# Second weights of two experts loaded by column halves, output stored by halves and in larger pieces

## The chip, the cores and the metric

The kernel runs on one core of one Trainium2 chip. A core has five engines with their own instruction streams: TensorE (PE; its weight loads are listed as PEld), VectorE (DVE), ScalarE (ACT), GpSimd (POOL) and SyncE (SP). Transfers between the chip's memory (HBM) and the core's SBUF are run by 16 DMA engines; POOL issues this kernel's loads (queue q0 in the profile), SP its stores (queue q1). TensorE writes to PSUM, which has eight banks of 128 partitions x 2 KB.

The metric is the device time of one execution in microseconds. "Before" is a median of three runs.

## The reference

Two stages, on float32 inputs.

```python
# attention: q, k, v are (8, 8, 576, 64)
scores = scale * q @ k.T                  # per batch and head
scores = where(masks[head], scores, -1e9) # heads 0-3: last 32 positions
attn = softmax(scores)                    # heads 4-7: every 4th of the last 128
x = (attn @ v).transpose(0, 2, 1, 3).reshape(4608, 512)

# soft mixture of experts: phi (512, 32), w1 (8, 512, 1024), w2 (8, 1024, 512)
logits = x @ phi                          # 32 slots, 4 for each of 8 experts
slot_input = softmax(logits, axis=0).T @ x
for e in range(8):
    h = np.maximum(slot_input[e] @ w1[e], 0.0)
    slot_out[e] = h @ w2[e]               # (4, 512)
out = softmax(logits, axis=1) @ slot_out  # (4608, 512) float32
```

Every slot's input is a sum over all 4608 tokens, and every output row needs all 32 rows of `slot_out`. So the last stage, `out`, can begin only when attention is done for all tokens and the last expert's `w2` has been used. Columns of `out` depend on the same columns of `w2` alone.

## The kernel before

The kernel doesn't write its instructions in their final order. It describes operations (`op`), each with its engine, what it reads and writes, an estimated cost and a key, and a planner (`Prog.schedule`, L149) places them: on PE, ACT and DVE by the earliest possible start in its own model of time and, among starts within 0.12 us of each other, by key; on POOL and SP in the order in which they were described. Each engine then works through its list in order and waits on semaphores. The planner's model has one line for all transfers, in which each takes its bytes over 424 GB/s after those placed before. In the modelled stretch `FILL` it fills PE's gaps with matmuls of no use (L1022).

Attention runs in eight units, each two batches by four heads; its code is not touched. During it POOL loads q, k and v, and, as their buffers come free, the weights: `w1` of experts 0 to 6 into `WD`, then `w17`, `w20` to `w24` into the three staging buffers `stg`, then `w25`, `w26` and `w27` into `TT` (`wload`, L428; L766 to L768). A weight is 2 MB of float32 and is written as 1 MB of bf16: 128 partitions with 8 KB each, for `w2` eight chunks of 512 columns. A load may be split into parts by chunks, each with a semaphore of its own: `w27` is split at chunks 4, 6 and 7. After the weights come fifteen transfers of a few bytes (`mk`, L773).

After attention: `fo` and `siT` (the slot inputs, L785), the first layer into `h_sb` (L805 to L815), its transpose `hT` (L823), the row sums of the tokens' weights and their reciprocals `rtok` (L842, L847). `expT` holds the 4608 tokens' exponentials, token by column, with the 32 slots in 4 groups of 8 rows at partitions 0, 32, 64 and 96.

The second layer, `ffn2` (L880), adds into the PSUM pair `sp_`, one bank for each half of 256 columns: experts 0 to 3, 4 to 6, chunks 0 to 3 and 4 to 5 of expert 7, each for half 0 and then half 1. The sum so far, without chunks 6 and 7 of expert 7, is scaled into `so_sb` by DVE (L906) and ACT (L910). For the first 512 tokens the output starts from this incomplete sum (L941), and the missing chunks are added by matmuls with `G` (L943), which holds those tokens' weights times the hidden values of chunks 6 and 7, computed beforehand (L859 to L873). Meanwhile `ffn2` adds chunks 6 and 7 for all others; the complete slot output is `so_all`: POOL copies rows 0 to 95 from `so_sb` (L913), DVE and ACT scale rows 96 to 127 (L962, L966).

The output goes by groups of 256 tokens, partition p taking tokens 2p and 2p + 1 of the group: two matmuls of 512 columns into a PSUM pair (L990), one evacuation with scaling by `rtok` on ACT (L1002) and one on DVE (L1001), into buffers of weights no longer needed, and one store of 512 KB by SP (L977). The first group is evacuated and stored as two stores of 256 KB. In memory a partition's share of a store is one run of 4 KB (2 KB in the first group).

Of the kernel before, what the change touches and what calls it, by code (L numbers as in the profile page):

```python
# [65 lines left out]
class Pool:  # L66
# [38 lines left out]
    def use(self, tile, op):  # L105
        for i in tile.phys:
            self.last[i].append(op)
# [194 lines left out]
def bass_dilated_sliding_attn__then__soft_moe_slots_kernel(  # L302
# [45 lines left out]
    so_sb = sb("so_sb", [128, DM])  # L348
    m7 = sb("m7", [128, 1], F32)
# [6 lines left out]
    psum = Pool(8, {1: [[6]] + one[:6], 2: [[0, 1], [2, 3], [4, 5], [6, 7]]})  # L356
# [40 lines left out]
    b_m7, b_soa = Buf(), [Buf(), Buf(), Buf()]  # L397
# [24 lines left out]
    def home(ap, al, name):  # L422
        b = Buf()
        b.al = al
        HOME[name] = (ap, b)
        b_home.append((ap, b))

    def wload(name, parts=((0, 8),)):  # L428
        ap, b = HOME[name]
        e = int(name[2:])  # L430
        src = (moe_w1 if name[:2] == "w1" else moe_w2)[e]
        c = 4 if name[:2] == "w1" else 8
        v_ = src.rearrange("(p c) f -> p c f", c=c)
        d_ = ap.rearrange("p (c f) -> p c f", c=c)
        b.parts = []
        for i, (lo, hi) in enumerate(parts):
            lo_, hi_ = lo * c // 8, hi * c // 8
            sem = DmaSem(nc, f"s_{name}_{i}")
            pb = Buf()
            for al in b.al:  # L440
                pb.prev = pb.prev + al.ready + al.reads
            o = op("pool", lambda g, lo_=lo_, hi_=hi_: [g.dma_start(d_[:, lo_:hi_], v_[:, lo_:hi_])],  # L442
                   after=pb.prev, a=[pb], cost=0.6, sem=sem, nbytes=2097152 * (hi - lo) // 8)
            b.parts.append((lo, hi, pb))
            b.ready.append(o)
# [321 lines left out]
    wload("w26")  # L767
    wload("w27", ((0, 4), (4, 6), (6, 7), (7, 8)))  # L768
# [66 lines left out]
    NOG = N_TOK // 256  # L835
    tok = [expT[:, 256 * o:256 * o + 256].rearrange("p (t j) -> p j t", j=2) for o in range(NOG)]
    rs = tile(psum, 1)

    def rsum(t):
        for o in range(NOG):  # L840
            for j in range(2):
                i_ = t.matmul(bank(rs)[:, 2 * o + j:2 * o + j + 1], tok[o][:, j], rowm[:],  # L842
                              start=True, stop=True)
        return i_
    op("pe", rsum, r=b_expT + [b_rowm], w=[rs], alloc=[rs], cost=1.0, key=K1 + 1,
       after=[ffn1])
    op("dve", lambda vv: vv.reciprocal(rtok[:], bank(rs)[:, 0:2 * NOG]), r=[rs], w=[b_rtok],  # L847
# [6 lines left out]
    h7, t_soa = tile(pPT), tile(pPT)  # L854
    G = [tile(pPT), tile(pPT)]

    def so_all(p0=0, p1=128, sl=slice(0, 512)):
        return sbt(t_soa)[p0:p1, sl]
# [16 lines left out]
    sp_ = tile(psum, 2)  # L875
    b_sp = [Buf(), Buf()]

    chain = []

    def ffn2(es_, lo, hi_, h_, key):  # L880
        pbs = [pb for e in es_ for l2, h2, pb in HOME[f"w2{e}"][1].parts
               if l2 < hi_ and h2 > lo]

        def pe(t):
            for cc in range(lo, hi_):
                for e in es_:
                    j, hi = e % 4, e // 4
                    i_ = t.matmul(pair(sp_)[32 * j:32 * j + 32, h_, 0:256],
                                  hT[:, hi, cc, j, :],
                                  w2v[e][:, cc, 256 * h_:256 * h_ + 256],  # L890
# [3 lines left out]
        o = op("pe", pe, r=[b_hT[0], b_hT[1]] + pbs, alloc=[] if chain else [sp_],  # L894
               a=[sp_, b_sp[h_]], cost=0.12 * (hi_ - lo), mode="c", key=key, after=chain[-1:])
# [4 lines left out]
    for es_, lo, hi_ in (((0, 1, 2, 3), 0, 8), ((4, 5, 6), 0, 8), ((7,), 0, 4), ((7,), 4, 6)):  # L900
        for h_ in range(2):
            ffn2(es_, lo, hi_, h_, K1 + 2 + es_[0] + 0.1 * lo + 0.02 * h_)
    for h_ in range(2):
        sl = slice(256 * h_, 256 * h_ + 256)
        if h_ == 0:
            op("dve", lambda vv, sl=sl: vv.tensor_scalar(so_sb[:, sl], pair(sp_)[:, 0, 0:256],  # L906
                                                         rcs[:, 0:1], None, op0=AluOp.mult),
               r=[b_sp[0], b_rcs, sp_], w=[b_so[0]], cost=0.35, key=K1 + 20)
        else:
            op("act", lambda ac, sl=sl: ac.activation(so_sb[:, sl], pair(sp_)[:, 1, 0:256],  # L910
                                                      ACTF.Copy, scale=rcs[:, 0:1]),
               r=[b_sp[1], b_rcs, sp_], w=[b_so[1]], cost=0.4, key=K1 + 20)
    op("pool", lambda g: g.tensor_copy(so_all(0, 96), so_sb[0:96, :]), r=b_so, w=[b_soa[0], t_soa],  # L913
       alloc=[t_soa], cost=1.0, key=K1 + 21)

    osts = []
    for ap, b in b_home[:9]:
        t32 = ap.bitcast(F32).rearrange("p (n j f) -> p n j f", n=2, j=2)
        for n_ in range(2):
            osts.append((t32[:, n_], b))  # L920

    PO = []
    NGT = NG // 256

    def Gt(o, c):
        return sbt(G[c])[:, 256 * o:256 * o + 256].rearrange("p (t j) -> p j t", j=2)
    pb7 = {l2: pb for l2, h2, pb in HOME["w27"][1].parts}
    PO = [[tile(psum, 2), tile(psum, 2)], tile(psum, 2)]
    head = {}

    def first(c, key):
        for o in range(2):
            for j in range(2):
                po = PO[0][j] if o == 0 else PO[1]

                def pe(t, o=o, j=j, po=po):
# [138 lines left out]
```

## Time and profile before

| What | Value |
|---|---|
| median of three runs (lowest, highest) | 182.53 us (182.01, 182.73) |
| span of the profiled execution | 180.5 us |
| busy: PE, DVE, ACT, POOL | 133.5, 114.9, 93.7, 44.9 us |
| read from HBM, written to HBM | 61.94 MB, 9.44 MB |
| loads, 100 to 136 us: written to SBUF | 216 GB/s |
| stores, 158 to 178 us | 405 GB/s |
| granted TensorE clock, mean | 0.956 |

The span is from the first to the last instruction of one profiled execution. The runs are timed around the whole launch, so they are longer by what lies before the first and after the last instruction; the profiled execution has no such time of its own, and its span is what stands beside the runs. The load rate counts the bf16 bytes that are written; the float32 bytes read are twice as many. These rows are from the costliest groups of instructions (line, engine, operation, out<-in, shape, count | busy us, mean ns | idle before) between 150 and 181 us:

```profile
L1001 DVE TENSOR_SCALAR WD<-ps,rtok 128x512 f32<-128x512 f32 x13 | 8.7, 740 | 0.8 <-PE ps L943 0.8
```

```profile
L1002 ACT ACTIVATE WD<-ps,rtok 128x512 f32<-128x512 f32 x13 | 7.6, 725 | 0.8 <-PE ps L943 0.8
L1002 ACT ACTIVATE stg<-ps,rtok 128x512 f32<-128x512 f32 x4 | 2.6, 728 | 0.0
```

### The profile page before, as it was taken

To read this page: it belongs to the slowest core of one execution; us is meant where nothing else is said; L and a number is where in the kernel's file an instruction comes from. 1 tells how busy PE (TensorE), PEld (TensorE's weight loads), DVE (VectorE), ACT (ScalarE), POOL (GpSimd) and SP (SyncE) were. 2 spreads that over 40 slices of the span, in tenths; PEclk is the share of its full clock that TensorE was granted. 3 is DMA by queue.
4 is the path that set the end of the run, shared out by engine and by line. 5 is a ranking of instruction groups with operands and counts; after the bars stand their busy time and mean duration, and the time that the engine had idled before them with its cause. 6 is when DMAs were issued, how large, how long until landed. Compare 5 with 4: busy or idle time off the path is not lost.

```text
span 180.5 us, 5811 instructions
## 1 busy us (share of the span) xinstructions
PE 133.5 (74%) x2597; PEld 99.2 (55%) x2597; DVE 114.9 (64%) x263; ACT 93.7 (52%) x138; POOL 44.9 (25%) x90
## 2 busy tenths in 40 slices
PE   0019769967988989888986898798999966995000
PEld 0019659656768767568865677775646654411000
DVE  6840495894797798688699179789840501799000
ACT  2004867945767975675975374874410301797000
POOL 7990702501600701700200200016970001000000
PEclk9999999999999999999999699999999999999655
DMA  5999999999999999999999999999999993499998
GB/s 72 196 219 206 220 210 212 218 212 216 214 214 219 211 216 214 214 216 212 216 213 212 218 214 218 216 216 214 212 221 212 216 188 53 155 404 406 403 406 318
DMA packets 8808, 40.81 MB, mean 226 GB/s; under 512 B 2384, under 2 KB 2640, under 8 KB 5328
## 3 DMA queue, kind: packets, MB, share of 16 engines
q0 software_dynamic: 5520, 30.94, 83.5%
q1 hardware_dynamic: 3264, 9.50, 13.5%
q8 instruction: 20, 0.33, 0.7%
q14 instruction: 4, 0.03, 0.0%
HBM read 61.94 MB, written 9.44 MB: 395 GB/s over the span
## 4 chain that ended last, share of the span: by engine, by line
PE 31%; DVE 26%; DMA 19%; ACT 9%; issue 4%; POOL 2%; DVEq 0%; POOLq 0%
DMA TT<-in_moe_w_dram 14%; DVE XB L644 7%; DVE PT L594 7%; PE ps L542 6%; DMA stg<-in_v_dram 5%; DVE WD L1001 5%; PE ps L537 5%; PE ps L688 4%; ACT TT L561 4%; ACT PT L586 4%; DVE VN L609 4%; PE ps L604 4%; PE ps L661 3%; PE ps L579 3%; PE ps L633 3%
## 5 line engine op out<-in xcount | busy, mean ns | idle before, releaser
L561 ACT ACTIVATE TT<-ps 128x864 f32<-128x864 f32 x32 | 28.6, 895 | 32.0 <-PE ps L542 23.1
L586 ACT ACTIVATE PT<-ps 128x768 bf16<-128x768 f32 x48 | 36.6, 815 | 6.3 <-PE ps L579 5.9
L644 DVE TENSOR_TENSOR XB<-ps,RV 96x768 bf16<-96x768 f32 x32 | 30.3, 947 | 0.7
L542 PE MATMUL ps<-ident,stg 96*64 96x96 bf16 x576 | 17.9, 225 | 17.1 <-DMA stg<-in_v_dram 13.0
L542 PEld LDWEIGHTS ps<-ident,stg 96*64 96x64 bf16 x576 | 15.8, 124 | 18.6 <-DMA stg<-in_v_dram 13.0
L609 DVE COPY VN<-ps 128x768 bf16<-128x768 bf16 x32 | 17.5, 547 | 10.5 <-PE ps L604 10.5
L413 POOL DMA_DIRECT2D stg<-in_q_dram x16 | 8.5, 536 | 44.5 <-PE ps L542 23.8
L633 PE MATMUL ps<-VN,PT 128*128 128x65 bf16 x384 | 17.7, 194 | 2.0 <-DVE PT L594 0.9
L673 DVE COPY XT<-ps 128x576 bf16<-128x576 bf16 x17 | 10.1, 597 | 12.2 <-PE ps L661 12.2
L604 PE MATMUL ps<-ident,TT 128*128 128x128 bf16 x192 | 16.5, 221 | 1.9 <-issue 1.1
L633 PEld LDWEIGHTS ps<-VN,PT 128*128 128x128 bf16 x384 | 14.5, 98 | 4.4 <-DVE PT L594 1.7
L579 PE MATMUL ps<-TT 64*128 64x96 bf16 x384 | 15.2, 204 | 1.9 <-ACT TT L561 1.0
L661 PE MATMUL ps<-ident,XB 96*128 96x96 bf16 x192 | 12.9, 208 | 3.2 <-DVE XB L644 3.0
L537 PE MATMUL ps<-ident,stg 96*128 96x96 bf16 x288 | 14.9, 206 | 0.1
L604 PEld LDWEIGHTS ps<-ident,TT 128*128 128x128 bf16 x192 | 11.0, 98 | 5.9 <-issue 2.6
L594 DVE TENSOR_TENSOR PT<-PT,mask_d 128x768 bf16<-128x768 bf16 x24 | 13.0, 544 | 0.9 <-ACT PT L586 0.4
L537 PEld LDWEIGHTS ps<-ident,stg 96*128 96x128 bf16 x288 | 13.0, 98 | 0.3 <-ACT PT L586 0.3
L661 PEld LDWEIGHTS ps<-ident,XB 96*128 96x128 bf16 x192 | 9.8, 99 | 6.0 <-DVE XB L644 4.9
L442 POOL DMA_DIRECT2D stg<-in_moe_w_dram x6 | 3.2, 534 | 39.4 <-PE ps L537 26.4
L579 PEld LDWEIGHTS ps<-TT 64*128 64x128 bf16 x384 | 9.6, 94 | 5.9 <-ACT TT L561 1.1
L594 DVE TENSOR_TENSOR PT<-PT,mask_p 128x768 bf16<-128x768 bf16 x24 | 12.6, 538 | 0.0
L674 ACT ACTIVATE XT<-ps 128x576 bf16<-128x576 bf16 x15 | 9.7, 649 | 3.7 <-PE ps L661 3.5
(92 smaller groups left out, 193.5 us busy)
## 6 DMA issues: line engine op xcount, KB each, us to landing
WD<-in_moe_w_dram POOLq DMA_DIRECT2D x7, 1024.0 KB, 28.0
out_dram<-WD SPq DMA_DIRECT2D x13, 512.0 KB, 5.0
stg<-in_moe_w_dram POOLq DMA_DIRECT2D x6, 1024.0 KB, 23.1
stg<-in_q_dram POOLq DMA_DIRECT2D x16, 288.0 KB, 17.9
stg<-in_k_dram POOLq DMA_DIRECT2D x16, 288.0 KB, 19.7
stg<-in_v_dram POOLq DMA_DIRECT2D x16, 288.0 KB, 21.6
TT<-in_moe_w_dram POOLq DMA_DIRECT2D x2, 1024.0 KB, 20.8
out_dram<-stg SPq DMA_DIRECT2D x4, 512.0 KB, 5.1
```

The costliest lines, as they stand in the source:

```text
L537: i_ = t.transpose(bankb2(pt, a)[:, 96 * kk:96 * kk + 96], two[:, j // 2, c, :], ident[0:96, 0:96])
L542: i_ = t.transpose(bankb2(pt, a)[64 * hx:64 * hx + 64, 96 * kk:96 * kk + 96], src[:, hx, c, :], ident[0:96, 0:96])
L561: return ac.activation(d, sv, ACTF.Copy)
L579: i_ = t.matmul(pair(sc)[:, hx, QB * x:QB * x + QB], win(u, 1, h01, blk_, bpar)[64 * hx:64 * hx + 64], win(u, 0, h01, blk_, bpar)[64 * hx: ...
L586: op("act", lambda ac: ac.activation(sbt(pt)[:, 0:768].rearrange("p (x n) -> p x n", x=2), pair(sc)[:, :, 0:384], ACTF.Exp, scale=SCALE), ...
L594: return dv.tensor_tensor(p_, p_, m.unsqueeze(1).to_broadcast([128, 2, 384]), AluOp.mult)
L604: i_ = t.transpose(bankb(pv)[:, 128 * m:128 * m + 128], win(u, 2, h01, m, bpar), ident[:, :])
L609: op("dve", lambda dv: dv.tensor_copy(sbt(vn)[:, :, :, 0:64], bankb(pv)[:, 0:768].rearrange("p (m x d) -> p m x d", m=6, x=2)), r=[pv], w= ...
L633: i_ = t.matmul(pair(po)[:, bk, 65 * po_:65 * po_ + 65], sbt(pts[i])[:, o_:o_ + 128], sbt(vn)[:, m, half, 0:65], start=True, stop=True)
L644: op("dve", lambda dv: dv.tensor_tensor(sbt(xb)[:].rearrange("p m (x h d) -> p h x m d", x=2, h=2)[:, h01], pv()[:, :, :, 0:64], sbt(rv)[: ...
L661: i_ = t.transpose(bankb(px)[:, QB * m:QB * m + QB], sbt(xb)[:, m, 128 * x:128 * x + 128], ident[0:QB, 0:QB])
L673: return en.tensor_copy(d, s_)
```

## The change

`w26` and `w27` are loaded by column halves: first columns 0 to 255 of `w26`, then of `w27` (chunks 0 to 5, then 6 to 7), then the same for columns 256 to 511. A part now names chunks and columns, and `ffn2` waits for the parts that meet its own.

The order of the second layer is experts 0 to 3 and 4 to 5 for both halves, then expert 6 and chunks 0 to 5 of expert 7 for half 0, then `half(0, ...)`, then the same for half 1. `half` scales the sum so far into `so_sb`, makes the output of the first 512 tokens as before (incomplete sum, then `G`), adds chunks 6 and 7, completes `so_all` for its columns, and evacuates and stores its 256 columns of the first six groups of 256 tokens (`NAB = 6`). The remaining 3072 tokens go at full width in groups of 512, 512, 1024 and 1024, one store each; a partition then takes 4 or 8 tokens in a row.

In the half stores a partition's share is two runs of 1 KB; in the others it is one run of 8 or 16 KB. In the loads by halves a chunk is a run of 1 KB that is read and 512 B that are written. `so_all` lies in the bytes of `psA_sb` in place of a tile of the `PT` ring, and bank 7 of PSUM joins the single banks. Stores of the first part are issued by SP in the order half 0, groups 0 to 5, half 1, groups 0 to 5.

```diff
-    wload("w26")
-    wload("w27", ((0, 4), (4, 6), (6, 7), (7, 8)))
+    for h_ in range(2):
+        sl = (256 * h_, 256 * h_ + 256)
+        wload("w26", ((0, 8) + sl,))
+        wload("w27", ((0, 6) + sl, (6, 8) + sl))
...
+    NAB = 6
+    GRP = [2] * NAB + [4, 4, 8, 8]
...
-    for es_, lo, hi_ in (((0, 1, 2, 3), 0, 8), ((4, 5, 6), 0, 8), ((7,), 0, 4), ((7,), 4, 6)):
...
+    def half(h_, key):
+        sl = CH[h_]
+        eA, eB = (("dve", "act"), ("act", "dve"))[h_]
+        xe = op(eA, lambda en: scaled(en, so_sb[:, sl], bank(sp_[h_])[:, 0:256], rcs[:, 0:1]),
+           r=[b_sp[h_], b_rcs, sp_[h_]], w=[b_so[h_]], cost=0.45, key=key)
+        op("pool", lambda g: g.tensor_copy(so_all(0, 96, sl), so_sb[0:96, sl]), r=[b_so[h_]],
+           w=[b_soah[h_][0]], after=b_psA.ready + b_psA.reads, cost=0.6, key=key + 0.1)
+        po = [tile(psum, 1) for _ in range(3)]
...
+        for c in (None, 0, 1):
+            for o in range(2):
+                for j in range(2):
...
+                        if c is None:
+                            return t.matmul(d_, row(d0, 2)[j], so_sb[:, sl],
...
+                        return t.matmul(d_, sbt(G[c])[:, d0 + j:d0 + 256:2], w2v[7][:, 6 + c, sl],
+                                        start=False, stop=c == 1, skip_group_check=True)
...
+        ffn2((7,), 6, 8, h_, key + 3.5, after=[xe])
...
+        for j in range(2):
+            op(("act", "dve")[j], lambda en, j=j: scaled(
+                en, AB[0][1][:, j, sl], bank(po[j])[:, 0:256], rtok[:, j:j + 1]),
+               r=[po[j], b_rtok], a=[ob], after=prev, cost=0.4, key=key + 4)
+        store(d0, 2, ap, ob, key + 4, h_)
+        op(eB, lambda en: scaled(en, so_all(96, 128, sl), bank(sp_[h_])[96:128, 0:256],
+                                 rcs[96:128, 0:1]),
...
+        for o in range(1, NAB):
...
+                    for j in range(2):
+                        i_ = t.matmul(bank(p2)[:, CH[j]], row(d0, 2)[j], so_all(0, 128, sl),
+                                      start=j == 0, stop=True, skip_group_check=True)
...
+            kr = rtok[:, 2 * o:2 * o + 2].unsqueeze(2).to_broadcast([128, 2, 256])
...
+                return dv.tensor_tensor(ap[:, :, sl], bank(p2).rearrange("p (j f) -> p j f", j=2),
+                                        kr, AluOp.mult)
+            if o % 2 == 0 or o == 1:
+                op("dve", evd, r=[p2, b_rtok], a=[ob], after=prev, cost=0.65, key=key + 4 + o)
+            else:
+                for j in range(2):
+                    op("act", lambda en, ap=ap, p2=p2, j=j, o=o: scaled(
+                        en, ap[:, j, sl], bank(p2)[:, CH[j]], rtok[:, 2 * o + j:2 * o + j + 1]),
+                       r=[p2, b_rtok], a=[ob], after=prev, cost=0.4, key=key + 4 + o)
+            store(d0, 2, ap, ob, key + 4 + o, h_)
+
+    for es_ in ((0, 1, 2, 3), (4, 5)):
+        for h_ in range(2):
+            ffn2(es_, 0, 8, h_, K1 + 2 + es_[0] + 0.02 * h_)
+    ffn2((6,), 0, 8, 0, K1 + 10)
+    ffn2((7,), 0, 6, 0, K1 + 11)
+    half(0, K1 + 20)
+    ffn2((6,), 0, 8, 1, K1 + 30)
+    ffn2((7,), 0, 6, 1, K1 + 31)
+    half(1, K1 + 40)
+
+    for i, (n, hs) in enumerate(((4, (3,)), (4, (4,)), (8, (5, 6)), (8, (7, 8)))):
...
+        for j0 in range(0, n, 2):
+            po = tile(psum, 2)
...
+                for j in range(2):
+                    i_ = t.matmul(pair(po)[:, j, :], row(d0, n)[j0 + j], so_all(), start=True, stop=True)
...
+            for j in range(2):
+                op(("act", "dve")[j], lambda en, ap=ap, po=po, j=j, j0=j0, n0=n0: scaled(
+                    en, ap[:, j0 + j, :], pair(po)[:, j, :], rtok[:, n0 + j0 + j:n0 + j0 + j + 1]),
+                   r=[po, b_rtok], a=[ob], after=prev, cost=0.6, key=key)
+        store(d0, n, ap, ob, K1 + 70 + 10 * i)
```

## The prediction

> **What bounds the kernel now.** I read the page's 40 slices first, because two rows there answer the question by themselves.
>
> ```profile
> DMA  5999999999999999999999999999999993499998
> GB/s 72 196 219 206 220 210 212 218 212 216 214 214 219 211 216 214 214 216 212 216 213 212 218 214 218 216 216 214 212 221 212 216 188 53 155 404 406 403 406 318
> ```
>
> The DMA row is full from slice 1 to 32 (loads; GB/s counts the bf16 bytes that are written, half of the f32 bytes read) and again from slice 35 on (stores, 404 GB/s). Between them is one hole. The kernel is a stream of transfers, so a change is worth what it does to that hole and to the work in the stream. A table of 1 us stretches shows the hole's size (columns: PE, PEld, DVE, ACT, POOL busy, clock, DMA share, GB/s):
>
> ```profile
> 148.00:149.00 1.00, 1.00 (x36) 0.95 (x30) 0.00 (x0) 0.00 (x0) 0.00 (x0) 1.00 0.96 144
> 149.00:150.00 1.00, 0.47 (x14) 0.18 (x6) 0.00 (x0) 0.00 (x0) 0.00 (x0) 1.00 0.59 99
> 150.00:151.00 1.00, 0.91 (x8) 0.57 (x6) 0.00 (x0) 0.00 (x0) 0.00 (x0) 1.00 0.72 103
> 151.00:152.00 1.00, 0.61 (x4) 0.30 (x4) 0.20 (x1) 0.20 (x1) 0.00 (x0) 1.00 0.20 20
> ...
> 154.00:155.00 1.00, 1.00 (x7) 0.45 (x6) 0.97 (x3) 0.97 (x3) 0.00 (x0) 1.00 0.00 0
> 155.00:156.00 1.00, 1.00 (x6) 0.49 (x5) 0.24 (x2) 0.17 (x2) 0.00 (x0) 1.00 0.86 324
> 156.00:157.00 1.00, 1.00 (x7) 0.42 (x5) 1.00 (x2) 1.00 (x2) 0.00 (x0) 1.00 0.53 201
> 157.00:158.00 1.00, 1.00 (x5) 0.24 (x4) 1.00 (x3) 1.00 (x3) 0.00 (x0) 1.00 0.47 193
> 158.00:159.00 1.00, 0.94 (x4) 0.23 (x4) 1.00 (x2) 1.00 (x3) 0.00 (x0) 1.00 1.04 418
> ```
>
> Missing share, from 148 to 158: 0.04 + 0.41 + 0.28 + 0.80 + 0.98 + 1.00 + 1.00 + 0.14 + 0.47 + 0.53 = 5.7 us. That is the most that filling it could give. What makes it is the chain of work between the last weights and the first store, in order of time:
>
> ```profile
> 151.15 0.61 PE L888 MATMUL ps<-TT,hT 128*32 128x256 bf16 x4 [0.24 <-DMA TT<-in_moe_w_dram]
> ...
> 151.80 0.48 DVE L906 TENSOR_SCALAR so_sb<-ps,rcs 128x256 bf16<-128x256 f32 x1 [7.40 <-PE ps L888]
> ...
> 152.43 0.60 PE L941 MATMUL ps<-so_sb,expT 128*128 128x256 bf16 x4 [0.67 <-DVE so_sb L906]
> ...
> 152.86 1.04 PE L943 MATMUL ps<-TT,PT 128*128 128x256 bf16 x8
> ...
> 153.72 0.88 DVE L1001 TENSOR_SCALAR WD<-ps,rtok 128x256 f32<-128x256 f32 x2 [1.44 <-PE ps L943]
> ...
> 154.29 16.68 SPq L977 DMA_DIRECT2D out_dram<-WD  x15
> ```
>
> From the landing at 151.10 (PE goes at 151.15) to the first store's issue at 154.29 is 3.2 us; its first packet follows at 155.14 (+0.85), its landing at 156.35.
>
> **The slow engine's ledger.** The landing records hold 16 increments for each transfer, one for each DMA engine. In the loads the engines have drifted apart: w25 is complete on the first at 138.57 and on the last at 141.73, the last part of w27 on 148.47 and 152.38. A consumer waits for the last, so I keep the books of the slowest engine: w25 done 141.73, loads done 152.38, the fifteen tiny mk transfers (0.17 us apart) until 154.93, stores from 155.14. For it most of the 5.7 us is not idle: a gap of at most 2.8 us (152.38 to 155.14) and about 0.9 us around 157, 3.7 us in all. Its end closes: the third store's first packet at 157.53 + 17 stores x 1.287 us + 0.6 us from last packet to landing = 180.0; measured 180.04, and the span ends 0.46 us later.
>
> **Part 1: column halves of the weights.** Removed: 8 packets of 8192 B on each engine for w26, and 8 of 4096, 8 of 2048, 16 of 1024 for w27 (sizes as written). Added: 256 packets of 512 B (2 MB / 512 / 16 engines), in six transfers for five. No packet of 512 B stands in the trace. On the first engine the spacing of landings is 4.88, 2.44, 1.25 and 0.66 us for 8 packets of 8192, 4096, 2048 and 1024 B: 610, 305, 156, 82 ns a packet, a line of 0.072 ns/B and 8 ns. At 512 B the line gives 45 ns, and 42 without the completion write (a 4-byte record of 22 ns for each group of 8, rare among 64); I take 43. Bounds: 38 ns (the 8192 B rate, no cost), and 60 ns from the packets' recorded durations (98, 173, 324, 625 ns, which overlap their neighbours by 15 ns; the line goes to 60). Loads: 256 x 43 = 11.0 us for 9.9 (4.88 + 2.44 + 1.25 + 2 x 0.66), +1.1; bounds -0.1 to +5.5. The Trainium skill ("Advanced Engine Details and Errata", Clock Domains) has 42 to 43 ns for a descriptor of 1 KiB, which is what each of these reads; by that the sum is 10.9 us, and no run here shows it yet. POOL issues 22 transfers instead of 21, at the 0.5 us of its rows; it is idle from 134 to 152 and the data are 14 us behind the issues, which hides slower issuing too. If it did not, each us late would delay the loads by one.
>
> **Part 2: stores by halves, and larger ones.** Twelve stores of 256 KB in 1 KB pieces: 192 packets an engine. Stores of 2048 and 4096 B record 86 and 164 ns (0.038 ns/B and 9 ns): 47 ns at 1 KB, 9.0 us. Bounds: 41 ns (rate of 4096 B), 7.9 us, and 86 ns (a piece of 1 KB as dear as one of 2 KB), 16.5 us; I take the line, since 128 B packets of phi record 13 ns, near it. The rest, 3072 tokens, has pieces of 8 and 16 KB: 8 x (2 x 315 + 2 x 620) ns = 15.0 us for 12 x 1.287 = 15.4; bounds 14.9 and 15.4. Before, all stores took 2 x 0.69 + 17 x 1.287 = 23.3 us; after, 24.0. The Trainium skill ("Trace Analysis", DMA Optimizations) speaks against this part: transfers under 2 KB carry a significant overhead and should be batched. In "DMA: Bandwidth & Descriptors" (Anatomy of one DMA) it is priced as 2.0 us + bytes / 436 GB/s for each, 2.6 us for one of these and 31 us for twelve in a row. The trace's own pair of 256 KB stores landed at 156.35 and 157.00, 0.65 us apart, so the 2 us overlap here and the row decides.
>
> **Part 3: compute that moves.** The first half's chain now starts when w27's chunks 0 to 6 of columns 0 to 256 have landed. It is the old chain: two more L888 matmuls (0.2 us), the 0.48 us scaling, 4 + 8 matmuls, one 0.48 us evacuation: 3.4 us. The six groups' evacuations are, on DVE, one 128x256 (0.48) and three 128x512 by tensor_tensor (not in the trace on this shape; between the 740 ns of L1001 and the 947 ns of L644's 96x768), on ACT 128x256 pieces at 0.47: about 3 us a half, against 4.5 us of transfer: hidden. If it were not, each us would be a us of empty queue, once a half. The GpSimd copy (0.61 us for 512 columns) is done twice, beside the evacuations. From then on a pair of tiles costs 0.74 us against 1.25 us of transfer, hidden.
>
> **The sum, slow engine.** Half 0 of the loads: 141.73 + 5.5 + 0.4 (half of the 0.75 us by which the last engine's loads exceeded the first's) = 147.6, chunks 0 to 6 at 146.9. First store issued 150.3, first packet 151.15. Of half 1's 5.9 us, 2.35 are then left, 1.6 of chunks 0 to 6. How an engine shares itself between the load queue and the store queue no row shows: bounds are that the loads lose nothing, and that they wait for all of the half-0 stores (4.5 us); I take turns about, packets being of like cost. Then chunks 0 to 6 land at 151.15 + 2 x 1.6 = 154.35, all at 155.85, and of the 4.5 us of half-0 stores 2.15 are left, until 158.0. The second chain ends in a first packet at 154.35 + 3.4 + 0.85 = 158.6: a hole of 0.6 us remains where 3.7 were. Then 4.5 + 15.0 = 19.5 us: 178.1, + 0.6 landing + 0.4 = **span 179.1**, 1.4 below 180.5. The median of the runs, 182.53, is 2.0 above the profiled span; I keep that difference: **181.1 us**. Check as a difference: holes -3.1, loads +1.1, stores +0.7 = -1.3. With the loads losing nothing the hole closes and the time is 180.5; with loads waiting for all stores, chunks 0 to 6 land at 157.25, first packet 161.5, span 182.0, time 184.0.
>
> **Rivals.** *Nothing measurable.* PE takes its work in the planner's order. Where that puts the half-1 matmuls of experts 6 and 7 ahead of groups 2 to 5 of half 0, those four wait for the half-1 landing; PE already waits so at 147.41 and 149.86 before L888. Then only two stores run beside the loads, which land (chunks 0 to 6) near 154.1; the four come 1 us of matmuls and evacuation later, first packet 156.2 (+0.85), run until 159.2, then 19.5 + 1.0: span 179.7, time 181.7. For it: the planner's transfers never share an engine, so it expects half 1 early. Against: it also counts each group as ready about when the weights are.
>
> *Slower: the 512 B packet.* Place: half 1 of the loads. If a packet costs the recorded 60 ns, half 0 takes 7.7 + 0.4 us, chunks 0 to 6 land at 148.8, the first store packet at 153.05; 3.9 us of half-1 chunks 0 to 6 remain and by turns land at 160.85; by then the half-0 stores are almost used up, the queue is empty from 162 to 165.1, and 165.1 + 19.5 + 1.0 = span 185.6, time 187.6. Between 43 and 60 ns the end moves 0.38 us a ns, so the sign turns near 47 ns, and half a per cent is lost from 49 ns on. For it: the recorded durations, and every added packet lies ahead of the chain. Against: the spacing of four sizes, on one line. Loads that wait for the stores (184.0) have the same end by another way.
>
> *More than forecast.* Pieces of 512 B and 1 KB at the large pieces' rate: loads 9.8, stores 7.9 + 14.9: 1.1 + 1.2 us less, and half 0 0.6 us earlier: about 178.8.
>
> **How the numbers follow.** About 0.5% (0.9 us) can be told from no change, so faster means below 181.6 and slower above 183.4. Forecast with its near bounds (180.3 to 181.6) 0.48, more than forecast 0.09, nothing measurable 0.19, slower 0.24. Faster 0.57, same 0.19, slower 0.24. The forecast's own range is 179.8 to 181.6; the range that should hold 8 in 10 runs from the cheap pieces, 178.8, to a packet of 50 ns or loads held up by the stores, 184.0.
>
> **What would show it.** Right: 512 B load packets 43 to 46 ns apart on an engine; first store issued near 150.3; the DMA share near 1 from 151 on with less than 1 us missing near 158; stores of 1 KB pieces at about 340 GB/s, large ones at 410. Wrong: first store later than 152, a second hole of 3 us near 160, SP issues of half-0 groups bunched after the half-1 landing, or DVE and ACT setting the store spacing. Only a load packet above 47 ns, or stores that hold the loads off, would make me wrong in sign.

## The result and the profile after

The changed kernel takes **179.94 us** (median of 4 runs, 179.31 to 180.75) beside 182.41 us for the kernel before on the same chip: ratio 0.988, 95% interval 0.9859 to 0.9902, so 1.2% faster. The forecast was 181.1 us in a range of 178.8 to 184.0. The profiled execution has a span of 179.0 us, where 179.1 was predicted; its own time, 180.75, is the highest of the four. The record gives every execution's time and span, the profiled one's too; over all runs here they differ by 1.67 to 1.81 us. Of e8_order_no_mk and e11_early_order_no_mk below, the profiled execution is likewise one of the longest (182.45 and 182.41 us at medians of 179.9 and 179.52): those two traces are read for what happened inside them, not against other traces.

The 40 slices of the changed kernel, the two rows shown before:

```profile
DMA  5999999999999999999999999999999999889996
GB/s 81 192 216 212 216 214 212 222 214 212 219 210 210 217 214 217 208 226 207 220 208 220 211 216 222 212 211 223 212 211 213 194 198 118 251 293 396 421 458 293
```

The slices with 3 and 4 tenths are gone; what is left of the hole is thin and spread over two slices (8 and 8). The same stretch in steps of 1 us (PE, PEld, DVE, ACT, POOL busy, clock, DMA share, GB/s):

```profile
149.00:150.00 1.00, 1.00 (x10) 0.35 (x6) 0.48 (x1) 0.00 (x0) 0.04 (x1) 1.00 0.96 118
150.00:151.00 1.00, 1.00 (x11) 0.90 (x11) 0.00 (x0) 0.18 (x1) 0.35 (x1) 1.00 0.77 111
151.00:152.00 1.00, 1.00 (x12) 0.72 (x11) 0.96 (x2) 0.50 (x2) 0.00 (x0) 1.00 0.50 52
152.00:153.00 1.00, 1.00 (x10) 0.72 (x9) 0.38 (x2) 0.26 (x2) 0.00 (x0) 1.00 0.48 75
153.00:154.00 1.00, 1.00 (x10) 0.60 (x8) 1.00 (x2) 1.00 (x3) 0.00 (x0) 1.00 1.00 268
154.00:155.00 1.00, 0.17 (x3) 0.02 (x2) 0.07 (x1) 0.93 (x3) 0.01 (x1) 1.00 0.75 255
...
158.00:159.00 1.00, 1.00 (x10) 0.72 (x8) 0.79 (x2) 0.57 (x2) 0.00 (x0) 1.00 1.05 354
159.00:160.00 1.00, 0.94 (x5) 0.37 (x4) 1.00 (x2) 1.00 (x4) 0.00 (x0) 1.00 0.44 153
160.00:161.00 1.00, 1.00 (x6) 0.43 (x4) 1.00 (x3) 1.00 (x3) 0.00 (x0) 1.00 0.88 293
```

Missing share, counted as in the prediction: 0.04 + 0.23 + 0.50 + 0.52 + 0.25 + 0.56 + 0.12 = 2.2 us, where 5.7 were missing before. At 151 to 153 the rate is only 52 and 75 GB/s: engines that are done with their loads wait for the first stores (the first is issued at 151.55, its first packet starts at 152.81), while the others still work on loads and mk. A second, smaller hole has opened at 159. The chain of waits, in order of time, shows what makes both:

```profile
145.08 4.29 PE ps L901 x110
149.37 0.75 PE ps L1052 x3
150.12 0.44 PE ps L957 x4
150.56 0.87 PE ps L960 x8
151.43 0.98 PE ps L901 x10
152.42 0.56 PE ps L989 x4
152.97 0.02 issue
153.00 1.57 ACT WD L932 x4
154.57 0.38 ACT so_sb L932
...
156.07 0.48 DVE WD L931
156.56 0.64 DVE WD L998
157.20 0.03 issue
157.23 0.50 DVE psA_sb L931
157.74 0.05 issue
157.78 0.41 PE ps L989 x2
158.19 0.02 issue
158.21 1.29 DVE WD L998 x2
```

Before, this chain began with a DMA (`TT<-in_moe_w_dram`, then L888). In this execution no DMA stands in it: PE works through 110 matmuls of the second layer without a pause, though the half-0 weights had landed by 147.7. Two waits are of one kind: the engine has other evacuations ahead. `so_sb` of half 1 waits until ACT is done with four evacuations of half 0 (153.00 to 154.57), and rows 96 to 127 of `so_all` (`psA_sb` L931, 157.23) wait for a DVE that evacuates L998 first. SP's stores begin at 151.55 (154.29 before):

```profile
151.55 1.27 SPq L926 DMA_DIRECT2D out_dram<-WD  x2
```

The evacuations between 150 and 181 us, from the groups of instructions, are near the rows they were priced by, except that the two-column evacuation by tensor_tensor is cheaper, 689 ns:

```profile
L931 DVE TENSOR_SCALAR WD<-ps,rtok 128x512 f32<-128x512 f32 x8 | 5.4, 744 | 0.0
L998 DVE TENSOR_TENSOR WD<-ps,rtok 128x512 f32<-128x512 f32 x6 | 4.0, 689 | 1.1 <-PE ps L989 1.1
```

```profile
L932 ACT ACTIVATE WD<-ps,rtok 128x256 f32<-128x256 f32 x10 | 4.1, 475 | 9.5 <-PE ps L960 6.7 <-PE ps L989 2.8
```

The landing records of the slowest DMA engine give the ledger (us; loads by their last part, mk by its last transfer). The records don't name the engine; that the last landing of each transfer is the same engine's is assumed, since from w25 to the last weights of the changed kernel the last is a steady 4.05 to 4.13 us behind the first.

```
                          before     after
w25                       141.73    142.34
w27 half 0, chunks 0 to 5    -      146.99
w27 half 0, all              -      147.72
w27 (half 1), 0 to 5      151.10    152.32
all loads                 152.38    153.06
mk                        154.93    155.90
first store issued        154.29    151.55
first store landed        156.35    156.10
last store landed         180.04    178.54
```

On this engine 25.1 us passed from the last mk to the end, now 22.6; of these 2.5 us it pays 1.0 for the later end of loads and mk (0.6 of it was there at w25 already). That is the 1.5 us between the spans.

### The profile page after: what moved, and what is told of

Its sections match the earlier page's. It is cut to its first block, busy times and chain, and to the rows that moved or that the text cites. A ratio compares the mean times of both kernels' runs of the same rounds, so it can differ in the third digit from the quotient of the medians.

```text
span 179.0 us, 5831 instructions
## 1 busy us (share of the span) xinstructions
PE 136.4 (76%) x2614; PEld 104.3 (58%) x2614; DVE 116.0 (65%) x264; ACT 94.1 (53%) x141; POOL 47.4 (26%) x92
## 4 chain that ended last, share of the span: by engine, by line
PE 47%; DVE 28%; ACT 9%; DMA 5%; issue 3%; POOL 1%; DVEq 0%; POOLq 0%
DVE XB L651 9%; PE ps L549 7%; DVE PT L601 7%; DMA stg<-in_v_dram 5%; PE ps L544 5%; PE ps L695 5%; PE ps L611 5%; ACT PT L593 4%; PE ps L668 4%; DVE VN L616 4%; PE ps L586 3%; DVE WD L931 3%; PE ps L1052 3%; PE ps L901 3%; ACT TT L568 3%
## 5 line engine op out<-in xcount | busy, mean ns | idle before, releaser
L611 PE MATMUL ps<-ident,TT 128*128 128x128 bf16 x192 | 17.7, 232 | 1.6 <-issue 0.9
L586 PE MATMUL ps<-TT 64*128 64x96 bf16 x384 | 15.8, 211 | 2.0 <-ACT TT L568 1.0
L611 PEld LDWEIGHTS ps<-ident,TT 128*128 128x128 bf16 x192 | 11.8, 103 | 5.9 <-issue 2.3
L932 ACT ACTIVATE WD<-ps,rtok 128x256 f32<-128x256 f32 (+1 forms) x18 | 8.7, 591 | 9.5 <-PE ps L960 6.7
L586 PEld LDWEIGHTS ps<-TT 64*128 64x128 bf16 x384 | 10.1, 97 | 6.1 <-issue 1.7
```

The source lines that it names most:

```text
L586: i_ = t.matmul(pair(sc)[:, hx, QB * x:QB * x + QB], win(u, 1, h01, blk_, bpar)[64 * hx:64 * hx + 64], win(u, 0, h01, blk_, bpar)[64 * hx: ...
L611: i_ = t.transpose(bankb(pv)[:, 128 * m:128 * m + 128], win(u, 2, h01, m, bpar), ident[:, :])
```

## The experiments

The expectations name their own theories. Where they speak of S and O: *overlap* (O) is the prediction's, the gain is half-0 stores moved into the hole, and loads and stores share an engine by turns. *Starved stores* (S) has it that the loads lose nothing; on an engine that still has loads or mk queued, stores wait for all of them. The reason for S was in the records of the changed kernel: its first store lands on the first engine at 153.89 and on the last at 156.10, 0.2 us after that engine's last mk.

**e1_small_rest: the last 3072 tokens in twelve stores of 512 KB.**

```diff
-    GRP = [2] * NAB + [4, 4, 8, 8]
+    GRP = [2] * NAB + [2] * 12
...
```

> The changed kernel, with the last 3072 tokens in twelve stores of 512 KB (runs of 4 KB) as before the change, instead of two of 1 MB and two of 2 MB. My theory (the hole is filled, and the larger stores give a little): a packet of 4096 B at 161 ns against 316 ns for 8192 and 616 for 16384 makes 12 x 1.29 = 15.4 us of 14.9, so 0.5 us slower than the changed kernel, ratio to the kernel before 0.990 to 0.992. Rival (the larger stores are the gain, the overlap gives nothing): all of the gain goes, ratio 0.998 to 1.003.

Measured: 180.42 us, ratio 0.9907 (0.9886 to 0.9929), beside 0.988 with large stores. The sign is as expected; the size, 0.5 us, is uncertain, since the two intervals overlap. Most of the gain is elsewhere, and the rival (all of it goes) is out.

**e2_half_loads: the kernel before, with only the loads by column halves.** Its compute order stays.

```diff
...
-    wload("w26")
-    wload("w27", ((0, 4), (4, 6), (6, 7), (7, 8)))
+    for h_ in range(2):
+        sl = (256 * h_, 256 * h_ + 256)
+        wload("w26", ((0, 8) + sl,))
+        wload("w27", ((0, 6) + sl, (6, 8) + sl))
...
```

> The kernel before, with only the column-half loads of experts 6 and 7 (second layer and stores in the old order). My theory: 256 packets of 512 B at 41.5 ns are 10.7 us for 9.9, +0.8; and the chain to the first store now starts 0.7 us before the last weights have landed where it started 1.3 before, +0.6; no store runs earlier. So +1.3 us, ratio 1.005 to 1.010. Rival (a 512 B packet costs its recorded 60 ns): +5.5 + 0.5 us, ratio about 1.03. Rival (the halves cost nothing): ratio 1.000 to 1.004.

Measured: 185.82 us, ratio 1.0169 (1.0126 to 1.0213): more than twice the expected loss (the profiled execution took 184.98 us). Its 1 us table (columns as above):

```profile
147.00:148.00 1.00, 0.53 (x3) 0.04 (x1) 0.00 (x0) 0.00 (x0) 0.00 (x0) 1.00 1.45 198
148.00:149.00 1.00, 0.00 (x0) 0.00 (x0) 0.00 (x0) 0.00 (x0) 0.00 (x0) 1.00 1.45 194
149.00:150.00 1.00, 0.00 (x0) 0.00 (x0) 0.00 (x0) 0.00 (x0) 0.00 (x0) 1.00 1.05 129
150.00:151.00 1.00, 0.40 (x12) 0.38 (x15) 0.00 (x0) 0.00 (x0) 0.00 (x0) 1.00 0.78 95
151.00:152.00 1.00, 1.00 (x23) 0.54 (x16) 0.00 (x0) 0.00 (x0) 0.00 (x0) 0.54 0.51 58
152.00:153.00 1.00, 0.50 (x6) 0.28 (x3) 0.00 (x0) 0.00 (x0) 0.00 (x0) 0.50 0.28 29
153.00:154.00 1.00, 1.00 (x6) 0.73 (x5) 0.00 (x0) 0.00 (x0) 0.00 (x0) 0.50 0.01 0
```

PE finds nothing to do for 0.47 + 1 + 1 + 0.60 = 3.07 us, and from 151 on its granted clock is 0.50, just as the chain to the first store begins. The weights it waits for land at 152.56 instead of 151.10 (+1.46, about the expected loss, but 0.51 of it was there at w25, ahead of the halves), and from there to the first issue it takes 4.46 us instead of 3.19 (+1.27). Together 2.73; the last store lands 2.76 later. The second term was in no one's sum. The chain of waits has it in the matmuls right behind the landing:

```profile
152.60 1.90 PE ps L895 x8
```

Before, these were four matmuls in 0.62 us. Here they are eight, because chunks 0 to 5 land as one part, and they run at half the clock; how much each of the two costs is not shown. So loads by halves alone lose.

**e3_large_stores: the kernel before, with only larger stores.** Groups of 2, 2, 4, 4, 8, 8 and 8 tokens a partition.

```diff
...
+    for i, (n, hs) in enumerate(((4, (1,)), (4, (2,)), (8, (3, 4)), (8, (5, 6)), (8, (7, 8)))):
...
+            op("pe", pe, r=b_soa + [t_soa] + b_expT, w=[po], alloc=[po], cost=0.45, key=key)
...
+        op("sp", lambda e, dst=dst, ap=ap: [e.dma_start(dst, ap)], r=[ob], cost=0.1, sem=so,
+           nbytes=262144 * n, key=K1 + 70 + 10 * i)
```

> The kernel before, with only the larger stores: the first 512 tokens as they were, then groups of 512, 512, 1024, 1024 and 1024 tokens with one store each. My theory: 19.85 us of packets instead of 16 x 1.29 = 20.6, -0.75 us, of which the wait for four tiles instead of two in front of the third store takes up to 0.7 back: ratio 0.996 to 1.000. Rival (the larger stores are the gain): -2 us or more, ratio 0.988 or less.

Measured: 181.15 us, ratio 0.994 (0.992 to 0.996): 1.0 us, somewhat more than expected. Packets of 8 and 16 KB record 311 and 615 ns; the last stores of 2 MB land 4.9 us apart, 428 GB/s, those of 512 KB in the kernel before 1.287 us apart, 407 GB/s. With e1 this puts the large stores' share of the gain at 0.5 to 1.0 us of 2.5.

**e4_pe_order: the changed kernel, with half 1's matmuls of experts 0 to 5 behind half 0's chain**, so that PE reaches the first chain sooner.

```diff
+    for h_ in range(2):
+        ffn2((0, 1, 2, 3), 0, 8, h_, K1 + 2 + 20 * h_)
+        ffn2((4, 5, 6), 0, 8, h_, K1 + 10 + 20 * h_)
+        ffn2((7,), 0, 6, h_, K1 + 11 + 20 * h_)
+        half(h_, K1 + 20 + 20 * h_)
...
```

> The changed kernel, with the second layer's matmuls of half 1 (experts 0 to 5) moved behind half 0's chain, and experts 4 to 6 in one group. In the changed kernel's trace chunks 0 to 6 of half 0 landed at 147.0 but so_sb was scaled at 149.4, since PE began the second layer at 145.0 and had both halves in front. My theory (PE is late, the transfers wait for it): so_sb scaled near 147.8, first store issued near 149.9 for 151.55; the share missing from the DMA engines between 149 and 153 (1.6 us) shrinks by about 1, time 0.5 to 1.2 us below the changed kernel, ratio 0.981 to 0.986. How an engine shares itself between loads and stores shows in the landing of half 1's chunks 0 to 6: 152.3 if the loads lose nothing, near 153.9 if by turns. Rival (the queue's slowest engine sets the end whatever PE does): ratio as for the changed kernel, 0.988.

Measured: 179.7 us, ratio 0.9865 (0.9843 to 0.9886). The first store is issued at 149.76 instead of 151.55, as expected, and still the end comes only 1.05 us earlier in the trace and 0.2 us in the medians. The first store packet starts at 151.02, and 100 load packets start after it. Still the two parts of w27's half 1 land at 152.05 and 152.76, 2.00 and 2.71 us behind w26's half 1; in e7 below, with no store packet before 154.37, it is 2.00 and 2.73. So the loads lose nothing, which speaks for S. The slowest engine is done with mk at 155.36 and then has stores without a break.

The order does not free half 0's groups of PE's work for half 1: 34 matmuls of L901 stand ahead of them, 32 of them half 1's.

```profile
149.65 1.20 PE ps L901 x34
```

**e5_no_mk: the changed kernel without the fifteen mk transfers.** They write a tile that nothing reads.

```diff
-    mk = sb("mk", [15, 136])
-    for n_ in range(1, 16):
-        o_ = sum(range(n_))
-        op("pool", lambda g, n_=n_, o_=o_: [g.dma_start(mk[0:n_, o_:o_ + n_], moe_w2[7, 0:n_, 0:n_])],
-           cost=0.3, sem=DmaSem(nc, f"s_mark{n_}"), nbytes=1024)
```

> The changed kernel without the fifteen tiny mk transfers behind the weights (nothing reads what they load). In the changed kernel's trace the slowest engine lands the last weights at 153.06, its last mk at 155.90 and the first store, issued at 151.55, only at 156.10; on the first engine mk ends at 151.62. Theory S (a DMA engine gives a store next to nothing until its load queue is empty, mk included, and the slowest engine sets the end): without mk the first store lands on the slowest engine near 153.6 and the end moves by 1.5 to 2.6 us, ratio to the kernel before 0.972 to 0.981. Theory T (the two queues take turns, and mk costs only its 0.4 us of packets an engine): ratio 0.984 to 0.988.

Measured: 180.0 us, ratio 0.9891 (0.9856 to 0.9926). The place is S's, the time is not: the first store lands on the slowest engine at 153.75 instead of 156.10, 0.7 us after its last load, but the median is where it was (in the trace the end comes 0.76 us earlier, beside the longest of the changed kernel's executions). The 1 us table shows why:

```profile
157.00:158.00 1.00, 0.96 (x9) 0.89 (x10) 0.53 (x1) 0.31 (x1) 0.00 (x0) 1.00 1.03 341
158.00:159.00 1.00, 0.94 (x5) 0.30 (x4) 1.00 (x3) 1.00 (x4) 0.00 (x0) 1.00 0.57 198
159.00:160.00 1.00, 1.00 (x6) 0.45 (x5) 1.00 (x3) 1.00 (x3) 0.00 (x0) 1.00 0.61 206
```

The stores of half 0 run out sooner, and the second hole grows to 0.43 + 0.39: what mk gave back waits for half 1's third store (issued at 158.19). From that issue to the last landing it is 19.59 us, and 19.61 in the changed kernel. The queue runs empty before that store, so its issue sets the end.

**e6_before_no_mk: the kernel before without mk** (the same edit).

> The kernel before without the mk transfers. There they end at 154.93 on the slowest engine, before the first store's first packet at 155.14. Theory S: they lie in the hole, so removing them gives nothing, ratio 0.998 to 1.002. Rival (mk slows the weights, or moving the issue queue matters): ratio below 0.995. Rival (mk pushes the weights out): the last weights land later, ratio above 1.004.

Measured: 182.15 us, ratio 0.9998 (0.9986 to 1.0009): nothing. There the first store was issued at 154.19, so its packets came when mk (done at 154.93 in the trace of before) was over anyway.

**e7_hold: the changed kernel, the stores of half 0 held by SP until the last weights have landed.**

```diff
...
+    hold = HOME["w27"][1].ready[-1:]
...
-        store(d0, 2, ap, ob, key + 4, h_)
+        store(d0, 2, ap, ob, key + 4, h_, hold if h_ == 0 else ())
```

> The changed kernel; SP waits with half 0's stores until the last part of w27 has landed (153.1 in place of 151.55 for the first issue). Theory S: the engines that finish their loads last don't run these stores before 155.9 in any case, so the end moves by 0 to 0.5 us: ratio 0.988 to 0.991. Rival O (stores run beside loads, and that overlap is the gain): 1.5 us or more are lost, ratio 0.996 or above.

Measured: 181.22 us, ratio 0.9938 (0.9922 to 0.9954), 1.1 us above the changed kernel by the ratios: between the two expectations, and decisive for neither. It does show that about that much of the gain is half 0's stores going out early. First store 153.11, half 1's third store 159.59, end 179.18: again 19.59 us after that issue.

**e8_order_no_mk: the edits of e4_pe_order and e5_no_mk together.**

> The PE order of the earlier run (half 1's matmuls of experts 0 to 5 behind half 0's chain; ratio 0.9865) and no mk transfers. Theory S: the earlier stores of that order, which waited for mk until 155.6 on the slowest engine, now run from 152.8 on; below the changed kernel without mk by up to 0.7 us, ratio 0.969 to 0.978. Theory T: ratio 0.982 to 0.986.

Measured: 179.9 us, ratio 0.9874 (0.9853 to 0.9896), not lower than e4 alone. In the profiled execution PE is idle for 2.0 us from 143.0 to 145.0, its clock is 0.56 at 146 to 147 and then 0.50, and the first store is issued at 152.15 instead of 149.76. With no work between, the earlier order meets the weights too soon in this execution; why the others, with a median of 179.9 us, are no faster than e4's is not shown. S's 0.969 to 0.978 was missed.

**e9_early_complete: chunks 6 and 7 and rows 96 to 127 of `so_all` done right behind `so_sb`**, scaling on DVE and rows on ACT in both halves: a shorter way to half 1's third store.

```diff
-        eA, eB = (("dve", "act"), ("act", "dve"))[h_]
+        eA, eB = "dve", "act"
...
+        ffn2((7,), 6, 8, h_, key + 0.2, after=[xe])
+        op(eB, lambda en: scaled(en, so_all(96, 128, sl), bank(sp_[h_])[96:128, 0:256],
+                                 rcs[96:128, 0:1]),
+           r=[b_sp[h_], b_rcs, sp_[h_]], w=[b_soah[h_][1]], after=b_psA.ready + b_psA.reads, cost=0.4, key=key + 0.3)
         po = [tile(psum, 1) for _ in range(3)]
...
```

> The changed kernel; in each half chunks 6 and 7 of expert 7 are added and rows 96 to 127 of so_all scaled (on ACT) right after so_sb is scaled (on DVE in both halves), before the matmuls of the first 512 tokens. Theory C: in every profile with the larger stores the end lies 19.6 us behind the issue of half 1's third store (158.93 and 178.54 in the changed kernel, 158.19 and 177.78 without mk, 159.59 and 179.18 with held stores), so the chain from half 1's weights to that store sets the end. It needs so_all, which here is ready 1.0 to 1.5 us sooner: third store of half 1 issued near 157.6, the end 0.7 to 1.3 us earlier, ratio to the kernel before 0.981 to 0.985. Theory S (the engine that finishes its loads and mk last sets the end): 0.987 to 0.989.

Measured: 179.69 us, ratio 0.9856 (0.9831 to 0.9882), above the expected 0.981 to 0.985. The chain did what was asked, half 1's third store is issued at 157.06 instead of 158.93, but the end is 20.4 us behind it instead of 19.6. On the slowest engine stores now follow mk (155.64) without a break, and the last lands 21.86 us after it.

**e10_early_order: the edits of e9 and e4 together.**

> The same early completion of so_all together with the PE order that has half 0 first (alone 0.9865). Theory C: half 1's third store near 156.5, ratio 0.977 to 0.982. Theory S: from this order on the slowest engine is busy without a gap from its last mk (155.4) to the end, so nothing is won over that order alone: 0.985 to 0.988.

Measured: 180.82 us, ratio 0.9911 (0.9886 to 0.9936): worse than either. The first store is issued at 151.38, 1.6 later than in e4, because 32 matmuls of half 1 were placed among those of the first chain; then one of SP's issues lasts 2.05 us (152.04 to 154.09) and the DMA share is 0.42 and 0.36 at 153 to 155. Why that issue took so long no row shows; e4 has one of 1.51 us (from 152.50).

**e11_early_order_no_mk: the edits of e9, e4 and e5 together.**

> The same without the mk transfers. If C and S each hold where the other's limit is gone, only this one wins in full: slowest engine done with loads at 152.8, then 23.2 us of stores and 0.6 to the last landing, 176.6, ratio 0.974 to 0.979. If mk is of no weight: as the run before it. Profiles in which PE waits for 2 us or more before half 0's matmuls may show a lower TensorE clock behind it and a late chain, as one without mk did.

Measured: 179.52 us, ratio 0.9842 (0.9818 to 0.9867), the lowest median of all, but above the expected 0.974 to 0.979 and within the interval of e9. In its profiled execution the clock is 0.50 from 147 to 153, and the first store is issued at 154.44.

**e12_early_no_mk: the edits of e9 and e5 together**, both limits lifted in the order of the changed kernel.

> The changed kernel with chunks 6 and 7 of expert 7 and rows 96 to 127 of so_all done right after so_sb (as in e9_early_complete), and without the fifteen small mk transfers. In e9 half 1's third store was issued at 157.06, but the run ended at 177.50, 20.4 us later instead of the 19.6 us of the runs with a hole, and 21.9 us after the slowest engine's last mk (155.64). Theory of two limits (the later of: issue of half 1's third store + 19.6 us; slowest engine's last load or mk + 21.9 us): without mk the slowest engine is free near 153.1, so the first limit decides: with the third store near 157.1 the last landing is near 176.8, span 177.2, ratio 0.979 to 0.985, lower than both e9 (0.9856) and e5_no_mk (0.9891). Rival, only the chain binds: as e9, 0.985 to 0.988, with e9's end not due to mk. Rival, only the engine's ledger binds: 153.1 + 21.9 = 175.0, span 175.4, ratio below 0.976.

Measured: 179.89 us, ratio 0.9881 (0.9838 to 0.9924), runs from 178.83 to 181.36. The interval holds the expected 0.979 to 0.985 only at its edge. The 1 us table of its trace:

```profile
152.00:153.00 1.00, 1.00 (x13) 0.73 (x13) 1.00 (x3) 1.00 (x3) 0.00 (x0) 1.00 0.20 43
153.00:154.00 1.00, 0.61 (x10) 0.30 (x4) 0.80 (x2) 0.57 (x2) 0.00 (x0) 1.00 1.05 344
154.00:155.00 1.00, 0.81 (x7) 0.56 (x8) 0.13 (x1) 0.38 (x1) 0.40 (x1) 1.00 1.05 347
...
158.00:159.00 1.00, 1.00 (x6) 0.62 (x6) 1.00 (x2) 1.00 (x3) 0.00 (x0) 1.00 1.05 345
159.00:160.00 1.00, 1.00 (x5) 0.22 (x3) 1.00 (x3) 1.00 (x3) 0.00 (x0) 1.00 1.04 335
```

From 153 on nothing is missing, neither at 154 (0.75 in the changed kernel) nor at 159. What is left is the end of the first hole (0.20 at 152). But the last store lands at 177.41 instead of 176.8, because a third limit decides: the first store was issued at 151.64, and all stores behind it take 25.77 us. In this trace the chain of waits up to that store goes through PE, which began the second layer only at 144.67 (141.75 in e9).

**The three limits.** Three quantities from each trace of the changed kernel and its variants with large stores (e8 and e11 left out): issue of the first store, issue of half 1's third store, and the slowest engine's last load or mk.

```
                 first    third    engine   last     19.6 after  21.9 after  25.8 after
                 store    of h. 1  free     landed   third       engine      first
after            151.55   158.93   155.90   178.54   178.5       177.8       177.4
e4_pe_order      149.76   157.55   155.36   177.49   177.2       177.3       175.6
e5_no_mk         150.80   158.19   153.06   177.78   177.8       175.0       176.6
e7_hold          153.11   159.59   155.63   179.18   179.2       177.5       178.9
e9_early_compl.  150.60   157.06   155.64   177.50   176.7       177.5       176.4
e10_early_order  151.38   158.16   155.65   178.53   177.8       177.6       177.2
e12_early_no_mk  151.64   157.36   152.91   177.41   177.0       174.8       177.4
```

The three distances were fitted on after, e9 and e12, one each; the largest of the three columns then gives the last landing within about 0.2 us for e4, e5 and e7, and misses e10 by 0.8, where an issue was held up. The two that were left out agree as well: 160.62 + 19.6 = 180.2 for 180.23 in e8, and 154.44 + 25.8 = 180.2 for 180.20 in e11, the only test of the third distance.

## Why the prediction was right, and where its steps were not

**What bounds it: right.** The stream of transfers with one hole at 148 to 158 was the right place to look, and filling it is where the time came from: 5.7 us of missing share became 2.2. e3 and e1 show that the rest of the gain is the large stores, and e7, which holds half 0's stores back, loses 1.1 us.

**Part 1, loads: right in price.** The 512 B packets record 60 ns and lie 41.6 ns apart on an engine, where 43 was taken and 38 and 60 were the ends. On the first engine w26 and w27 take 10.66 us for 256 of them instead of 9.90, +0.8 for the +1.1 predicted; on the slowest 10.7 to 11.3 in the runs by halves and 9.9 to 10.7 in those without. Half 0 landed at 146.99 and 147.72 for the predicted 146.9 (there called chunks 0 to 6, the upper end left out) and 147.6. POOL's issues of the parts took up to 0.90 us where 0.5 was taken, hidden as said: the first went out at 124.35 and landed at 144.99. The rule of the Trainium skill cited there ("Advanced Engine Details and Errata", Clock Domains: 42 to 43 ns) agrees with these 41.6. So the slower rival, a packet of 60 ns, is out; e2, slower by 1.7%, shows half of its mechanism: loads by halves alone do lose.

**Part 2, stores: right.** Packets of 1 KB record 46 ns and lie 48 apart in e12 (47 predicted), of 8 and 16 KB record 314 and 615 (315 and 620). In e12, where nothing interrupts them, the stores land over 177.41 - 154.18 = 23.2 us, plus 0.75 for the first: 24.0, as in the sum. The Trainium skill ("Perfetto Trace Analysis", DMA Optimizations) warns of transfers under 2 KB; these are pieces of 1 KB in transfers of 256 KB, and they do cost more by the byte, 46 ns a KB against 40 (161 ns for 4 KB). The 2.0 us for each transfer ("DMA: Bandwidth & Descriptors", Anatomy of one DMA) are that page's fit for transfers issued by GpSimd, while these are issued by SP; no such cost adds up here, queued half stores land 0.7 to 0.8 us apart.

**"I take turns about": this step failed.** Loads and stores do not share an engine by turns. Chunks 0 to 5 of half 1 landed at 152.32 instead of the predicted 154.35. In the changed kernel's trace the two hardly met: its last load packet starts before the first store packet (152.81); in e4, where they did meet, the weights landed at 152.05. The near bound, loads that lose nothing, was the truth. Its counterpart had been overlooked: the stores wait on each engine for its loads and for mk, which stands in the ledger before (152.38 to 154.93) and in no term of the sum. That brought 2 us for the second chain and cost the slowest engine 2.35 us of stores (first landing 156.10, and 153.75 without mk).

**First chain: a term was missing.** It was made to start when the weights land, at 146.9, and to put the first store at 150.3. In the profiled execution PE began the second layer at 145.01 and was busy with 110 matmuls of both halves until 149.37: 151.55. The sum has no term for PE's start. The 3.4 us from landing to issue are about right where PE is not late: e1, with the same order up to there, began at 141.37 and issued at 150.01, 3.04 us behind its weights (146.97), and e4, with another order, 3.05 behind. From issue to first packet it is 1.25 to 1.27 us in every trace with half stores, where 0.85 was taken from the stores before.

**Second chain: right to the first store, wrong to the third.** 3.4 us were taken from the landing to half 1's first store. It took 4.27 (152.32 to 156.59) in this trace, because PE, late here too, reached half 1's last matmuls only at 153.33, and `so_sb` then waited for ACT's evacuations of half 0 (the line at 153.00). Where PE was early it took 3.27 (e1), 3.41 (e4) and 3.38 (e9). What was left out in all of them is the third store. It needs `so_all`, which DVE finishes behind half 1's own first evacuations (the lines at 156.07, 156.56 and 157.23), so it is issued 2.1 to 2.35 us behind the first (after, e1, e4, e5, e7), while the two half stores between take 1.5. In e9 and e12, which finish `so_all` first, it is 1.25. "About 3 us a half, against 4.5 us of transfer: hidden" looked at the stores' rate only, not at the order on the engine. So a hole remained after all, at 159 instead of 158.

**The sum.** These errors nearly cancel: half 1's loads 2 us early, the first store 1.25 us late, the second chain 0.9 us long to its first store and more to its third, a hole of 0.7 us (0.56 + 0.12 of share) where 0.6 stood. That the span is 179.0 for 179.1 is luck. Of the signs that were named, the DMA share near 1 from 151 on did not come (0.50 and 0.48 at 151 to 153). The time, 181.1, was 1.2 above the median: 0.25 because time and span of one execution differ by 1.7 to 1.8 us, not the 2.0 taken from before's median and another execution's span, 0.8 because the profiled execution was the highest of four, and the 0.1 of the spans. *Nothing measurable*, through PE's order, was present in part: eight matmuls of half 1's expert 6 stand ahead of the groups of half 0 (among the ten at 151.43 in the chain). What they cost no run shows, since e4 puts 32 there. *More than forecast* (178.8) was not reached: the pieces cost what the line said.

**What stays open.** PE begins the second layer anywhere from 141.4 to 145.7 in the traces of kernels whose work up to there is the same, while the loads are steady (w25 done 141.6 to 142.5). In after (145.01), e5 (144.27) and e12 (144.67) that lateness reaches the first store; what causes it was not tried. No version was faster than the changed kernel by more than their intervals: e9, e4 and e11 (0.9856, 0.9865, 0.9842) are candidates, not results.

## What to carry to other kernels

When a tail of stores follows a chain of compute, write down the end as the latest of several sums, each an event plus the transfers that must follow it: here the first store, the first store behind a hole, and the time at which the slowest DMA engine is free. Removing one limit is worth only the distance to the next, a few tenths of a us here (e4, e5, e9), so read all of them before choosing an edit. A split that lets transfers start early also puts the first part's work ahead of the second part's on the engines that they share; price the second chain with that queue in front of it.

## What the runs showed of the hardware

- *Stores wait behind queued loads.* The loads lose nothing to stores: on the slowest engine the two parts of w27's half 1 land 2.00 and 2.71 us after w26's half 1 in e4, where 100 load packets start after the first store packet, and 2.00 and 2.73 in e7, where none does. The first store lands there 0.2 us after the last mk in the changed kernel and in e4 (155.36 and 155.57), and 0.7 us after the last load in e5, without mk. While mk are queued some store packets record up to 1181 ns where 46 is usual; in e5 and e12, without mk, none records over 75. The Trainium skill ("DMA: Bandwidth & Descriptors", Queues, rings and completion order) says that an engine goes round robin between the rings that have work; these records don't look like that.
- *A lagging engine catches up.* In the changed kernel the sixteen engines are 4.3 us apart at the last mk, 2.2 at the first store and 0.8 at the eighth; behind the hole, at the ninth, it is 0.24. The slowest lands seven stores in 4.30 us (156.10 to 160.40), 38 ns a packet of 1 KB, while in e12, with all engines in step, a packet takes 48 ns (8.43 us for eleven stores).
- *PE's clock drops after a short idle time.* 3.07 us idle in e2 and 2.0 us in e8 were followed by a granted clock of 0.50; 1.45 us of idle in the kernel before were not. Idle time alone does not decide, though: in the kernel before the clock also falls to 0.50 at 99.71, behind 3.41 us in which PE was busy for 2.07. The skill ("TensorE: Matmul & The Clock Gate", Part 1) puts the drop after at least one idle window of about 3.4 us; in these runs it came although PE was busy for part of such a stretch (0.49 of the 3.41 us ahead of the drop at 151.09 in e2).
